# X of steps 2 and 3 from TensorE products, the first six steps in a new order, and the early loads on SyncE's queue

## The chip, the cores and the metric

The kernel runs on one core of one Trainium2 chip. The metric is the time of one execution on the device in microseconds (us). The profile is that of one execution; its engines are named PE (TensorE), PEld (TensorE's weight loads), DVE (VectorE), ACT (ScalarE), POOL (GpSimd) and SP (SyncE, which here only issues transfers).

## What is computed

A delta-rule recurrence over 768 tokens for 4 batches of 8 heads of width 48, and an MLP with a hard-swish over its 3072 x 384 output.

```python
# q, k, v: (4, 8, 768, 48), beta: (4, 8, 768), all of them converted where they come as float64
k_n = k / (norm(k, axis=-1) + 1e-6)
for t in range(768):
    y[:, :, t] = q[:, :, t] @ state                       # (48) x (48 x 48), per batch and head
    state = state + beta_t * outer(k_n_t, v_t - k_n_t @ state)
x = y as (3072, 384)                                      # heads side by side
h = x @ w_in                                              # w_in 384 x 2048
out = (h * clip(h + 3, 0, 6) / 6) @ w_out                 # w_out 2048 x 384
```

q, k, v and beta are float32; the two weights are read as 64-bit numbers, in 16 pieces of 768 KB, and turned into float32 on the chip.

## The kernel before

**The recurrence in blocks.** A step takes 32 tokens of all four batches (128 partitions), so there are 24 steps. Within a step the recurrence is a triangular system. Its inverse, called X, is built from the strictly triangular products of the keys, and overwrites them in the tile LB. With X the step is a few small products, and only the state passes from step to step.

**What a step consists of.**
- `norms` (L337): the norms of the keys of a group of steps (sq, ss, root, some small operations, inv).
- `prep` (L378): GpSimd makes the normed keys kb (L383), the masks mb (L391) and the scaled keys bkb (L438); TensorE transposes keys and queries (pt, L409); ScalarE copies them to KQ (L412); TensorE multiplies them (sc, L425); VectorE masks the result into LB (L434).
- X, in one of two ways. `product` (L457) builds it from products on TensorE (pi, L485) with transposes, copies and sums between them on VectorE and ScalarE; it does one step, and takes TensorE's time. `inverse` (L551) takes a whole group of four steps to DRAM and back in another layout (A), eliminates column by column with 60 operations (pr, L566; A, L571), each needing the one before it, and brings X back through DRAM.
- `chain` (L601): ks (state times keys and queries, L622), R (L635), pz (X times R, L643), Z (L685), then su (the state's change, L710), py (L643), the new state (L726), y (L735), and in `seam` the transpose of y to xT (yt, L699).

**The MLP.** Two steps make a block of 256 tokens. `up` (L750) makes a unit of three products ph (L760) for each 128 columns of w_in, ScalarE's t (L765) and VectorE's g (L772). `down` (L788) makes products po with w_out (L795) for the first two blocks, `down_by_seven` (L836) a form with seven products for four for the others (L856). A piece of weights is converted by `scales` (five passes on ScalarE, L298) and `convert` (three on VectorE, L317, L322, L327) before it can be used. The converted pieces of w_in serve two units each.

**The order.** Everything is issued by hand. The string ORDER lists the first part as words: each word takes the next piece of one of the generators (p5 the next piece of step 5's prep, h2 of step 2's chain, x0 of step 0's product, i1 of group 1's inverse, n norms, k, q, v and w loads, a and c the two halves of a weight's conversion, u the next unit of the MLP, g VectorE's part of a unit that waits for it). All engines run their instructions in the order in which they are issued. From step 6 on a loop lays 15 units beside each step's chain and the preps of steps further on.

**Groups.** Steps 0 and 1 form group 0 and get X from `product`; steps 2 to 5 are group 1, 6 to 9 group 2, and so on up to 22 and 23; all these get X from `inverse` on VectorE. Before ORDER starts, the keys of six steps, queries of four, values of two and all pieces of w_in are issued, on SyncE's queue and partly on ScalarE's.

Of the kernel before, what the change touches and what calls it, by code (L numbers as in the profile page):

```python
# [22 lines left out]
n0*8 n1 p0 n1 p0 n1 p0 q*2 p0 q p1 q p1 n1 p0 p1 a n1 a*2 p0 q*2 a*2 c a q p1 x0 n1*2 a n1*3 a  # L23
p2*2 x0 q c k2 p2 a p1 p3 x1 c p3*2 p2 a x1*2 p2 p4 p1 a*2 x1 k2*2 p3 p2 a*3 p3 k2 p5 x0 c*2
k2*3 p3 x0 c a*4 x0 k2 c*3 p4 p5 k2*2 x1 k2 x0 p4 c*2 p5 p4 p5 p4*2 p5 x1*2 k2 x0 p5 a x1 a i1 c
x0 x1 a x0 c x1 k2 x1 x0*2 k2 c i1 v k2 i1 x1 i1 x0 i1*2 a i1*2 x0 q i1*3 a i1 h0*2 i1*3 q i1*3
h0 i1*3 v i1 x1 i1 q i1 h0 i1*3 a i1*2 a h1 a*2 h1 i1*2 h0 i1 h1 q h1 i1 c i1 v h1*2 v i1 h1 k2
i1*5 v i1 v i1 v c w v i1 a c a*2 i1 a i1 c i1 v q i1 a v*2 i1 v a c i1*4 w i1*2 h1 n2 i1*4 a
i1*3 a i1 h2 i1*2 c a i1 a i1 n2 a c*2 u a g c n2 a c u a n2 g u n2*3 a n2 q c a g n2*2 a c a p6
h2 u h2 c p6 a w p6 u q*2 a v g q*2 a h2 p6 c q*2 v u p7 a q p6 a q p7 p6 v p8 c g q h2 v h2 a c  # L30
w a p7 a k3 h3 u k3 p8 u a h2*2 k3 c g k3 g c h3 c h3 p8 a u k3 a k3 p7 u g q p8 u q w k3 p7 h3
a p9 p8 c a p9 k4 g p9 k4 p7 a*2 g u k3 k4 c k4 h3 a h3 p9 c w k3 k4 k3 a p9 g*2 h3 a c h4 k4 k3
u a h3 c g k4 h4 k3 c w u p8 k3*2 g k3 h4 k3 q a n3 a c n3 c a n3 u q u g u h4 a g p9 a c k4 h4
c a n3 a u a w k4 i2 w*2 a*2 u n3 a h4 v h5 h4 c a u c g n3 c n3*2 g v*2 u h4 n3 u v n3 u c p10
q a*2 q g k4 v q i2 p11 k4 u k4*4 p10 i2*2 q*2 i2*2 k4 u v i2*2 h5 v g h5 i2 a i2 q i2 p10 u h5
u v i2*2 q u i2*2 c i2 p10 g u i2 p10 i2*4 p11 p10 h5*2 q u q h5 p11 g u p11 i2 u i2*2 p12 i2 g
i2*2 p11*2 u i2*2 u i2*3 g i2 u*2 g i2 u*2 g u g u*2 g u i2*6 u*4 h5
# [4 lines left out]
def kernel(  # L42
# [34 lines left out]
    CB = 2  # L77
    TB = CB * P
    assert N % CB == 0 and CB <= GS

# [6 lines left out]
    NPC, NPM = 2, 4  # L87
    psC = ctx.enter_context(tc.tile_pool(name="psC", bufs=NPC, space=PSUM))
    psM = ctx.enter_context(tc.tile_pool(name="psM", bufs=NPM, space=PSUM))
# [43 lines left out]
    def load_k(t, eng=nc.sync):  # L133

        g, i = group(t)
        if i == 0:
            needs(*(("kb", first(g - 2) + j) for j in range(size(g - 2) if g >= 2 else 0)))
            kfs[g] = stage.tile([P, GS, H, D], FP32, name="kf", bufs=2)
        for b in range(B):
            eng.dma_start(out=kfs[g][rows(b), i], in_=tokens(k, b, t))  # L140
            if b == B - 1:
                past.add(("k", t))
            yield

    def load_q(t, eng=nc.sync):
        if t < N:
            if t >= NQB:
                needs(("qT", t - NQB))
            for b in range(B):
                eng.dma_start(out=qbufs[t % NQB][rows(b), :, 0:D], in_=tokens(q, b, t))  # L150
                if b == B - 1:
                    past.add(("q", t))
                yield
# [3 lines left out]
    def load_v(t):  # L157
        if t < N:
            if t >= NVF:
                needs(("R", t - NVF))  # L160
            vfs[t] = stage.tile([P, H, D], FP32, name="vf", bufs=NVF)
            for b in range(B):
                nc.sync.dma_start(out=vfs[t][rows(b)], in_=tokens(v, b, t))
                if b == B - 1:
                    past.add(("v", t))
                yield
# [61 lines left out]
    places = const.tile([128, 6], FP32, name="places")  # L228
    for i, value in enumerate((1152 - 7.5 / 16, -1600.0, -448.0, -704.0, 704.0 * 128, 1e-30)):
        nc.vector.memset(places[:, i : i + 1], value)  # L230
    powers = (
        (ACTF.Relu, 1.0 / 16), (ACTF.Abs, 1.0), (ACTF.Relu, 1.0), (ACTF.Abs, 1.0),
        (ACTF.Relu, -128.0),
    )
# [53 lines left out]
    def scales():  # L288

        for i in range(NW):  # L290
# [5 lines left out]
            d, z = raws[i], like(es[i % 2], i)  # L296
            for n, (func, scale) in enumerate(powers):
                nc.scalar.activation(  # L298
                    out=z, in_=z if n else d.bitcast(I16)[:, :, :, 3], func=func,
                    bias=places[:, n : n + 1], scale=scale,  # L300
                )
                if n == len(powers) - 1:
                    past.add(("scale", i))
                yield
# [32 lines left out]
    def norms(g, i0, n):  # L337
# [17 lines left out]
        nc.scalar.activation(out=root[:], in_=ss[:], func=ACTF.Sqrt, bias=places[:, 5:6])  # L355
# [14 lines left out]
        for i in range(n):  # L370
            invs[first(g) + i0 + i] = inv[:, i, :]
        yield
# [5 lines left out]
    def prep(t, dma):  # L378
# [3 lines left out]
        needs(*([("bkb", t - NKB)] if t >= NKB else []))  # L382
        nc.gpsimd.tensor_tensor(  # L383
# [17 lines left out]
        for j, src in enumerate((kb, qb)):  # L401
# [3 lines left out]
            ring("pm", NPM, ("pt", t, j))  # L405
            read(("pt", t, j))
            pt = psM.tile([128, NP, P], FP32, name="pt", tag="pm")
# [38 lines left out]
        if g > 0:  # L446
# [3 lines left out]
            dma.dma_start(  # L450
# [6 lines left out]
    def product(t, pool):  # L457
# [6 lines left out]
        needs(("bkb", t))  # L464
# [3 lines left out]
        VY = pool.tile([P, 2, H * C], FP32, name="VY", bufs=CB)  # L468
        V, Y = VY[:, 0, :], VY[:, 1, :]
        T = pool.tile([P, H * C], FP32, name="VT", bufs=CB)  # L470
        F = pool.tile([P, H * C], FP32, name="F", bufs=CB)
# [3 lines left out]
        def times(rhs):  # L475
# [3 lines left out]
            ring("pm", NPM, key)  # L479
            keys.append(key)  # L480
            ps = psM.tile([P, 2, H * C], FP32, name="pi", tag="pm")
# [69 lines left out]
    def inverse(g, dma, back):  # L551
# [5 lines left out]
        dma.dma_start(  # L557
# [4 lines left out]
        for j in range(1, C - 1):  # L562
# [3 lines left out]
            nc.vector.tensor_tensor(  # L566
# [4 lines left out]
            nc.vector.tensor_tensor(  # L571
# [3 lines left out]
        nc.vector.memset(A.rearrange("p c i -> p (c i)")[:, 0 : C * C : C + 1], -1.0)  # L575
        back.dma_start(
# [4 lines left out]
        for i in range(size(g)):  # L581
            yield
            LBv = LBs[first(g) + i][:].rearrange("p e a j w -> p (e a) j w")
            back.dma_start(out=LBv[:, :, 0, :], in_=x_dram[g][i].rearrange("h p c -> p h c"))
# [16 lines left out]
    def chain(t):  # L601
# [78 lines left out]
        ring("pm", NPM, ("pz", t))  # L680
        read(("pz", t))
        pz = psM.tile([P, 512], FP32, name="pz", tag="pm")
# [6 lines left out]
        def seam():  # L689

            blk, cc = divmod(t, CB)
# [3 lines left out]
            ring("pm", NPM, ("yt", t))  # L695
            read(("yt", t))
            pt = psM.tile([128, NKT, P], FP32, name="yt", tag="pm")
# [21 lines left out]
        ring("pm", NPM, ("py", t))  # L719
        py = psM.tile([P, 512], FP32, name="py", tag="pm")  # L720
# [29 lines left out]
    def up(blk):  # L750

        needs(*(("seam", blk * CB + i) for i in range(CB)))
        xT = xTs[blk]
        for f in range(NFC):
            needs(("w", f * 128 // WP))
            settle(2)
            ring("pm", NPM, ("ph", blk, f))
            ph = psM.tile([128, TB], FP32, name="ph", tag="pm")
# [23 lines left out]
    def to_dram(t, o):  # L782
        for b in range(B):
            r0 = b * S + t * C
            eng = nc.scalar if t >= N - CB and b % 2 else nc.sync
            eng.dma_start(out=out[r0 : r0 + C, :], in_=o[rows(b ^ 1)])

    def down(blk, c, f0):  # L788

        needs(("w", NWI + f0 // WF))  # L790
        if f0 == 0:
            ring("pm", NPM, ("po", blk, c))
            pos[c] = psM.tile([128, DM], FP32, name="po", tag="pm")
# [5 lines left out]
        if f0 + WF == NFC:  # L799
            if c == 0:  # L800
                pos["o"] = mlp[0].tile([128, CB, DM], FP32, name="o", bufs=1)
# [3 lines left out]
            to_dram(blk * CB + c, o)  # L805
# [14 lines left out]
    assert 2 * WP * NKT == HF * HM and CB == 2 and HF % 2 == 0  # L820
# [15 lines left out]
    def down_by_seven(blk):  # L836
# [8 lines left out]
        o = mlp[0].tile([128, CB, DM], FP32, name="o", bufs=1)  # L845
        u = mlp[0].tile([128, HM], FP32, name="u", bufs=1)[:]
        C11, C12, C21, C22 = (o[:, c, m : m + HM] for c in range(CB) for m in (0, HM))
# [264 lines left out]
```

## Time and profile before

| | |
|---|---|
| time, median of 3 | 724.28 us (723.74 to 726.2) |
| span of the profiled execution | 725.1 us |
| TensorE busy | 656.7 us (91%) |
| VectorE busy | 454.9 us (63%) |
| ScalarE busy | 247.3 us (34%) |
| GpSimd busy | 89.5 us (12%) |
| transfers | 44.72 MB, mean 62 GB/s |

The busy shares are means over a span whose beginning and rest differ much, so the questions are where TensorE is not busy, and what it waits for there. The profile gives for each instruction its start and its duration, and for the idle time before it the event that ended it. The clock that TensorE was granted is given per stretch, 1.00 being full speed.

### The profile page before, as it was taken

Reading aid. Unit: us, or ns where it says so; the run is one execution under the profiler, and the core shown is the slowest. Engines: PE = TensorE matmul, PEld = TensorE weight load, DVE = VectorE, ACT = ScalarE, POOL = GpSimd, SP = SyncE. Lnnn points to the kernel's source line nnn. Section 1 sums busy time; section 2 is a strip of 40 time slices with the busy share of each in tenths; the row PEclk is TensorE's granted clock in tenths of the full one; section 3 lists DMA queues with packets and bytes.
Section 4 is the critical chain, followed back from the end, with each engine's and each line's share of the span. In section 5 each row is a group of like instructions: output and inputs, shape, how many; then the busy total and the mean of one; then the engine's idle time right before and its main releaser. Section 6 shows DMA issues by size and latency. Waiting matters only on the chain.

```text
span 725.1 us, 25019 instructions
## 1 busy us (share of the span) xinstructions
PE 656.7 (91%) x10984; PEld 571.9 (79%) x10984; DVE 454.9 (63%) x1209; ACT 247.3 (34%) x467; POOL 89.5 (12%) x128
## 2 busy tenths in 40 slices
PE   0666839798979999999999999999999999999997
PEld 0455627666756789889889899898898898989997
DVE  6556996488583379665489464598444894533343
ACT  1763688593130331331322322322313213222130
POOL 3640024004031101041110031000000000000000
PEclk9966569899999999999999999999999999999999
DMA  7954437472042312421410411212302001000000
GB/s 135 298 119 89 112 91 176 90 183 37 8 96 48 75 32 42 90 36 26 96 32 15 98 33 31 52 21 60 53 2 50 13 16 39 2 24 1 23 1 22
DMA packets 135853, 44.72 MB, mean 62 GB/s; under 512 B 126112, under 2 KB 129184, under 8 KB 135744
## 3 DMA queue, kind: packets, MB, share of 16 engines
q1 hardware_dynamic: 126832, 40.99, 25.4%
q10 hardware_dynamic: 8912, 2.13, 1.5%
q8 instruction: 86, 1.41, 0.8%
q14 instruction: 23, 0.19, 0.1%
HBM read 32.60 MB, written 10.49 MB: 59 GB/s over the span
## 4 chain that ended last, share of the span: by engine, by line
PE 78%; issue 7%; DVE 5%; DMA 4%; POOL 2%; ACT 2%; SPq 1%; POOLq 0%; DVEq 0%
PE ph L760 31%; PE po L856 26%; PE po L795 3%; PE pz L643 3%; PE ks L622 3%; PE su L710 3%; PE py L643 3%; PE pt L409 3%; PE sc L425 2%; DMA kf<-in_k_dram 2%; DMA spare<-in_moe_w_in_dram 1%; PE pi L485 1%; ACT spare L298 1%; DMA vf<-in_v_dram 1%; PE yt L699 1%
## 5 line engine op out<-in xcount | busy, mean ns | idle before, releaser
L760 PE MATMUL ph<-xT,w_in 128*128 128x256 f32 x1152 | 269.6, 386 | 2.6 <-issue 2.3
L760 PEld LDWEIGHTS ph<-xT,w_in 128*128 128x128 f32 x1152 | 216.4, 193 | 34.7 <-issue 3.0
L765 ACT ACTIVATE t<-ph,halves 128x256 f32<-128x256 f32 x192 | 90.8, 474 | 207.3 <-PE ph L760 204.6
L772 DVE SCALAR_TENSOR_TENSOR g<-t,ph 128x256 f32<-128x256 f32 x192 | 79.8, 418 | 120.5 <-ACT t L765 120.3
L856 PE MATMUL po<-w_out,g 128*128 128x192 f32 x640 | 111.9, 327 | 0.0
L856 PEld LDWEIGHTS po<-w_out,g 128*128 128x128 f32 x640 | 104.2, 190 | 0.5
L856 PE MATMUL po<-spare,g 128*128 128x192 f32 x480 | 87.2, 330 | 0.0
L856 PEld LDWEIGHTS po<-spare,g 128*128 128x128 f32 x480 | 78.0, 190 | 1.2
L298 ACT ACTIVATE spare<-spare,places 128x768 uint16<-128x768 uint16 (+1 forms) x74 | 69.2, 940 | 7.7 <-DVE w_in L327 3.3
L566 DVE TENSOR_TENSOR pr<-A 128x30 f32<-128x30 f32 (+19 forms) x180 | 62.8, 349 | 4.1
L571 DVE TENSOR_TENSOR A<-A,pr 128x30 f32<-128x30 f32 (+19 forms) x180 | 61.9, 344 | 4.1
L842 DVE TENSOR_TENSOR g<-g 128x256 f32<-128x256 f32 x160 | 60.4, 428 | 3.7 <-PE po L856 3.5
L409 PE MATMUL pt<-ident,kb 128*128 128x128 f32 x96 | 18.3, 326 | 32.8 <-POOL kb L383 32.8
L795 PE MATMUL po<-w_out,g 128*128 128x384 f32 x128 | 45.4, 494 | 0.0
L383 POOL TENSOR_TENSOR kb<-kf,inv 128x384 f32<-128x384 f32 x24 | 23.5, 979 | 176.0 <-DVE inv L369 73.0
L412 ACT ACTIVATE KQ<-pt 128x512 f32<-128x512 f32 x48 | 28.2, 594 | 47.4 <-PE pt L409 47.4
L409 PEld LDWEIGHTS pt<-ident,kb 128*128 128x128 f32 x96 | 13.8, 167 | 36.0 <-POOL kb L383 33.8
L863 ACT ACTIVATE o<-po 128x192 f32<-128x192 f32 x40 | 13.2, 331 | 82.8 <-PE po L856 79.7
L391 POOL TENSOR_TENSOR mb<-beta_tok,mask 128x256 f32<-128x256 f32 x48 | 33.8, 724 | 56.2 <-DVE LB L434 56.2
L726 DVE TENSOR_TENSOR state<-state,su 128x384 f32<-128x384 f32 x46 | 23.3, 548 | 22.2 <-PE su L710 22.2
L795 PEld LDWEIGHTS po<-w_out,g 128*128 128x128 f32 x128 | 23.5, 192 | 12.9 <-issue 0.5
L635 DVE SCALAR_TENSOR_TENSOR R<-ks,parity,vf 128x192 f32<-128x192 f32 x46 | 16.9, 410 | 26.3 <-PE ks L622 26.2
(97 smaller groups left out, 581.5 us busy)
## 6 DMA issues: line engine op xcount, KB each, us to landing
spare<-in_moe_w_out_dram SPq DMA_DIRECT2D x8, 768.0 KB, 5.4
vf<-in_v_dram SPq DMA_DIRECT2D x96, 48.0 KB, 2.6
qb<-in_q_dram SPq DMA_DIRECT2D x92, 48.0 KB, 2.4
out_dram<-o SPq DMA_DIRECT2D x92, 48.0 KB, 1.6
kf<-in_k_dram SPq DMA_DIRECT2D x84, 48.0 KB, 2.8
w_out<-in_moe_w_in_dram SPq DMA_DIRECT2D x4, 768.0 KB, 9.6
LB<-x_dram SPq DMA_DIRECT2D x22, 128.0 KB, 3.1
x_dram<-A SPq DMA_DIRECT2D x5, 512.0 KB, 2.8
```

Source lines behind the costliest of these rows:

```text
L298: nc.scalar.activation(out=z, in_=z if n else d.bitcast(I16)[:, :, :, 3], func=func, bias=places[:, n : n + 1], scale=scale,)
L391: nc.gpsimd.tensor_tensor(out=mb[:, e], in0=beta_tok[:, t, e:H:2].unsqueeze(2).unsqueeze(3).to_broadcast([P, NP, 2, C]), in1=mask2[:].unsq ...
L409: nc.tensor.transpose(pt[:, p, :], src[:, 2 * p : 2 * p + 2].rearrange("p e w -> p (e w)"), ident[:])
L566: nc.vector.tensor_tensor(out=pv, in0=A[:, j, j + 1 :].unsqueeze(1).to_broadcast([n, j, w]), in1=A[:, 0:j, j].unsqueeze(2).to_broadcast([n ...
L571: nc.vector.tensor_tensor(out=A[:, 0:j, j + 1 :], in0=A[:, 0:j, j + 1 :], in1=pv, op=ALU.subtract)
L643: nc.tensor.matmul(ps[rows(place(b)), D * h : D * h + D], lhsT=m(h)[rows(b)], rhs=z[rows(b), D * h : D * h + D], start=True, stop=True, sk ...
L760: nc.tensor.matmul(ph[:], lhsT=w_in[:, s, f * 128 : (f + 1) * 128], rhs=xT[:, s, :], start=(s == 0), stop=(s == NKT - 1),)
L765: nc.scalar.activation(out=t1[:], in_=ph[:], func=ACTF.Relu, bias=half, scale=1.0 / 6.0)
L772: nc.vector.scalar_tensor_tensor(out=g, in0=t1[:], scalar=1.0, in1=ph[:], op0=ALU.min, op1=ALU.mult)
L795: nc.tensor.matmul(pos[c][:], lhsT=gs[blk, f // 2][:, f % 2, c * P : (c + 1) * P], rhs=w_out[:, f, :], start=(f == 0), stop=(f == NFC - 1),)
L842: nc.vector.tensor_tensor(out=A(f, *out), in0=A(f, *a), in1=A(f, *b), op=op)
L856: nc.tensor.matmul(ps[n][:], lhsT=A(f - f % 2, *a)[:, f % 2], rhs=b[:, f], start=(f == 0), stop=(f == HF - 1),)
```

## The change

Group 0 grows from two steps to four (CB 4; the MLP's blocks of two steps are now BK): steps 2 and 3 also get X from `product`. Groups are then 0 to 3, 4 to 7, 8 to 11 and so on, one fewer in all. The inverse of group 1 (steps 4 to 7) is done by GpSimd, the others by VectorE as before. ORDER is written anew; the loads that stood before it are words in it (q, k, v, w), in the order in which their data is used, on SyncE's queue, or on ScalarE's for a word in capitals (four of them). Norms of steps 0 and 1 are taken one step at a time (words m0, m1), and step 0's kb is made by VectorE. A weight's scale is made in three passes on ScalarE for five. Tiles of `product` have two buffers each; the first part has three PSUM banks in the place of four, and the fourth is set aside for products without a purpose that would fill TensorE's gaps (word z), of which this ORDER has none.

```diff
-    CB = 2
-    TB = CB * P
+    CB, BK = 4, 2
+    TB = BK * P
...
-    NPC, NPM = 2, 4
+    NPC = 2
...
+    psM, NPM = [None], [3]
...
-            for n, (func, scale) in enumerate(powers):
-                nc.scalar.activation(
-                    out=z, in_=z if n else d.bitcast(I16)[:, :, :, 3], func=func,
-                    bias=places[:, n : n + 1], scale=scale,
-                )
...
+            nc.scalar.activation(
+                out=z, in_=d.bitcast(I16)[:, :, :, 3], func=ACTF.Relu,
+                bias=places[:, 0:1], scale=1.0 / 16,
+            )
+            yield
+            nc.scalar.activation(
+                out=w, in_=z, func=ACTF.Prelu, bias=places[:, 1:2], scale=-1.0, alpha=TINY
+            )
+            yield
+            nc.scalar.activation(
+                out=z, in_=w, func=ACTF.Prelu, bias=places[:, 2:3], scale=-128.0 / TINY, alpha=TINY
+            )
...
-        nc.gpsimd.tensor_tensor(
+        (nc.vector if t == 0 else nc.gpsimd).tensor_tensor(
             out=kb[:, :, 0:D], in0=kfs[g][:, i],
...
-        VY = pool.tile([P, 2, H * C], FP32, name="VY", bufs=CB)
+        VY = pool.tile([P, 2, H * C], FP32, name="VY", bufs=2)
...
-    def inverse(g, dma, back):
+    def inverse(g, eng):
...
-            nc.vector.tensor_tensor(
+            eng.tensor_tensor(
                 out=pv, in0=A[:, j, j + 1 :].unsqueeze(1).to_broadcast([n, j, w]),
...
-            for t in range(LA):
-                drain(load_k(t, nc.scalar if t % 2 else nc.sync))
-                if t == 1:
-                    drain(load_q(0))
-                    drain(load_q(1, nc.scalar))
-            for t in range(CB, NQB):
-                drain(load_q(t))
-            for i in range(3):
-                load_w(i, early if i < 2 else stage)
-            for t in range(CB):
-                drain(load_v(t))
-            for i in range(3, NWI):
-                load_w(i)
...
+        return made(("i", g), lambda: inverse(g, nc.gpsimd if g == 1 else nc.vector), g < NG)
...
+            psM[0] = first_steps.enter_context(
+                tc.tile_pool(name="psM3", bufs=NPM[0], space=PSUM)
+            )
+            psI = first_steps.enter_context(tc.tile_pool(name="psI", bufs=1, space=PSUM))
+            idle.append(psI.tile([128, 128], FP32, name="idle"))
...
+                queue[0] = nc.scalar if word[0].isupper() else nc.sync
+                word = word.lower()
+                if word == "z":
+                    busy()
...
-            needs(("X", 0), ("X", 1), ("w", 0), ("w", 1))
+            needs(*(("X", t) for t in range(CB)), ("w", 0), ("w", 1))
```

The beginning of the new ORDER, up to the first transposes, and its first words around the first unit:

```
q K0 k0 q Q q k0 K0 w Q k0 q k0 m0 k0*2 m0*3 q m0 m1*7 q a m0*2 a p1 p0 c a k1 k0 q*2 c p1 c k1
...
p6 x3 x2 p6 c x3 a p6 x2 x3 a x2 v k3*2 p6 x3 x2 a c a x2 u g k2 q h2 c k2 k3 c u g i1 c h2 a k2
```

Lines of the changed kernel used below: pi is L498, pt L422, ph L773, and the two operations of the inverse are L579 and L584.

## The prediction

> **What bounds the kernel now.** I read the slices of the page first, then the busy times by stage, then TensorE's timeline at the edges of the stages.
>
> ```profile
> PE   0666839798979999999999999999999999999997
> ...
> PEclk9966569899999999999999999999999999999999
> ...
> L298 ACT ACTIVATE spare<-spare,places 128x768 uint16<-128x768 uint16 (+1 forms) x74 | 69.2, 940 | 7.7 <-DVE w_in L327 3.3
> ```
>
> A slice is 18.1 us. TensorE stands at nines from the thirteenth slice (217 us) on; before that it has gaps, and from 36 to 109 us its clock is 0.5 to 0.6. L298, ScalarE's passes over the weights (80 with all their forms, 0.94 us each), lies wholly in that early part. The stages, in the busy times by stretch:
>
> ```profile
> core 0: us, PE busy (x) PEld busy (x) DVE busy (x) ACT busy (x) POOL busy (x), PEclk, DMA share, GB/s
> 16.00:88.00 72.00, 47.95 (x1719) 40.58 (x1720) 50.69 (x112) 42.39 (x59) 20.72 (x24) 0.72 0.61 161
> 88.00:108.00 20.00, 7.44 (x32) 6.32 (x32) 19.05 (x50) 14.92 (x23) 3.08 (x4) 0.67 0.31 68
> 108.00:170.50 62.50, 54.28 (x1187) 42.34 (x1185) 41.89 (x84) 45.44 (x72) 16.42 (x21) 0.93 0.61 141
> 170.50:215.30 44.80, 41.16 (x523) 30.32 (x524) 32.77 (x86) 11.46 (x24) 8.98 (x11) 0.96 0.18 40
> 215.30:725.00 509.70, 505.89 (x7526) 452.34 (x7526) 301.29 (x836) 131.33 (x290) 36.51 (x48) 1.00 0.18 37
> ```
>
> From 215.3 on TensorE is busy 505.9 of 509.7 us at clock 1.00: that stage is its own work, and nothing outside it can shorten it. Before that, there is no product for 16 us, then 48 us of work in 72 at clock 0.72, 7.4 in 20, 54 in 62.5, 41 in 45: some 65 us idle, and part of the busy time is work at a slow clock. Time can be won or lost only here.
>
> ```profile
> 68.27 0.88 PE L643 MATMUL pz<-vf,LB 32*32 32x48 f32 x36 [1.70 <-DVE LB L543]
> ...
> 87.60 6.09 PE L760 MATMUL ph<-xT,w_in 128*128 128x256 f32 x24
> 106.25 1.11 PE L409 MATMUL pt<-ident,kb 128*128 128x128 f32 x4 [12.56 <-POOL kb L383]
> ...
> 113.27 0.60 PE L409 MATMUL pt<-ident,kb 128*128 128x128 f32 x4
> ...
> 215.32 0.94 PE L643 MATMUL pz<-R,LB 32*32 32x48 f32 x36 [3.36 <-DVE g L772]
> ```
>
> Columns: start, us, engine, line, operation, count, and in brackets the idle time before and what ended it. 68.27 is the first use of a finished X (step 0), 87.60 the first product with w_in; after its four units (a unit is three products, six records) TensorE stands 12.56 us for step 6's keys. 113.27 is the same four transposes as 106.25, 0.60 against 1.11 us: the clock. 215.32 is pz of step 6, the first step of the main loop.
>
> **The marker.** I counted TensorE's instructions in the two built orders up to pz of step 6. They are the same (52 + 52 transposes at pt, 384 sc, 96 ph, 36 po, and six steps of pz, su, py, ks, yt), save for pi: 384 before, 768 after. So the remaining 509.8 us hold for both, and the new time is (when pz of step 6 starts) + 509.8.
>
> [...]
>
> ```profile
> 66.32 0.19 DVE L571 TENSOR_TENSOR A<-A,pr 128x30 f32<-128x30 f32 x1
> ...
> 164.87 0.75 DVE L571 TENSOR_TENSOR A<-A,pr 128x30 f32<-128x30 f32 x1
> ```
>
> 0.19 us for the same instruction alone, 0.75 us beside GpSimd's kb and mb. GpSimd's own durations (min/median/max):
>
> ```profile
> L391 POOL TENSOR_TENSOR mb<-beta_tok,mask x48: 609/616/1324, 16.3 to 450.1; 128x256 f32<-128x256 f32 x48
> ```
>
> ```profile
> L383 POOL TENSOR_TENSOR kb<-kf,inv x24: 826/831/1424, 15.3 to 442.8; 128x384 f32<-128x384 f32 x24
> ```
>
> [...] a Prelu pass is taken at L298's 0.94 us. [...]
>
> ```profile
> 8.89 4.76 ACTq L140 DMA_DIRECT2D kf<-in_k_dram  x8
> 13.70 0.31 ACT L355 ACTIVATE root<-ss,places 128x16 f32<-128x16 f32 x1 [11.39 <-DMA kf<-in_k_dram]
> ```
>
> ScalarE issues eight key loads until 13.65 us, and the first root waits 11.39 us behind them.
>
> **The change part by part.**
>
> *Loads.* Twelve key and four query loads leave ScalarE's queue, four stay; loads come in order of use, weights later. ScalarE still issues beta until 3.4 us and then its four, so step 0's keys land near 7.5 us (issue 4.9 + 2.3, the landing of L140). Step 1's come behind one weight piece, near 9.5. Norms (sq 0.56, ss 0.55, root 0.31, five small ops of 0.2) give kb near 13 us, against 15.3. This is worth 2 to 3 us; bandwidth isn't the limit later (v of step 0 ends the first 5.5 MB; the kernel before had moved 5.6 MB by 30 us: 155 GB/s for 20, 336 and 165 for five each).
>
> *Scales.* 3 passes for 5: 48 for 80, so 32 x 0.94 = 30 us of ScalarE, in a stretch where it was busy 42 of 72 and 45 of 62 us. No path of its own; it shortens waits of pt and pi for ScalarE (2.9 + 2.8 + 1.4 us).
>
> *X of steps 0 and 1.* They start at 19 and 22 us (LB): four groups of transposes 4.3 us, KQ copies of 0.6, two sc of 1.2, LB 0.69. One product alone is 1.65 (four set-up ops) + 4 x 0.93 + 2 x 1.93 on TensorE + about 3.8 on VectorE and ScalarE + 11 hand-overs of 0.26 (the idle time of ScalarE between TensorE's pt and KQ) = 16 us. Two interleaved, with norms of steps 4 to 7 (5.8) and a conversion among them on VectorE, take about 22: first pz at 44.5, against 68.3, where other work stood between the parts.
>
> *From there to the first w_in product.* TensorE's new order holds, at the slow durations of this trace: the chains of steps 0 and 1 (pz 1.67, su 1.3, py 1.5, yt 0.9, and a ks of 1.96: 14.7 us), transposes of six steps (12 groups of 1.07: 12.9), six sc (7.2), and X of steps 2 and 3 (2 x 7.6 = 15.2): 50 us. VectorE has 38 us beside it. Following the waits by hand, instruction by instruction with these durations, gives 54 us; the profile shows a further 4.7 us of instruction supply before pi, and GpSimd's contention some 2. First unit at 44.5 + 60.5 = 105 (98 if neither shows, 113 to 119 if TensorE stays at its present share of 48 in 72). That is 17 us later than now, but with X of steps 0 to 3, preps of 0 to 7 and six to eight pieces of w_in done, so no hole of 12.56 us follows.
>
> *Units, step 2 on.* To pz of step 4: 26 units of 1.3 us, two chains of 3.9 at full clock, six groups of transposes of 0.5, two sc of 0.8: 46 us. VectorE has about 41 to 48 in the same stretch (20 g of 0.41, 19 conversion ops, two R/y, norms), so little stands.
>
> *X of steps 4 to 7 on GpSimd.* 60 dependent ops over 9920 columns. From 616 ns for 256 and 831 for 384: 0.19 + 1.68 ns a column, so 28 us; step 8's prep among them 2.9; times 1.18, the mean over the median of mb and kb (724/616, 979/831), 36.5; and hand-overs of 0.05 (0.4 us idle before the eight of L192): 40. Bounds: 31 with no contention, 55 if half of them take twice their time, as mb's maximum of 1324 does. It starts 8 us after step 6's LB (56.8 to 63.7 and the issue before it, in this trace), near 110, ends at 150. Behind it on GpSimd queue kb of steps 9 and 10, and TensorE's pt of step 9 stands before pz of step 4 in its order: due at 146 (105 + 41), released at 150, 4 us of wait. The way back through DRAM is 5.9 us (96.42 to 102.3), so pz of step 4 at 156 instead of 151. What VectorE gains: 21 us that stood at 66 to 97.
>
> *Step 5 and 6.* One unit and two sc cover little of the chain pz, Z, su, state, ks, R: 8 us, pz of step 5 at 164. Then 23 units (29.8) and 4.9 of chain and transposes: 35. VectorE has 36 before R of step 6 (50 ops of the next inverse 16.4, ten g, nine conversions) with GpSimd's preps against it, which stretch small two-input ops as shown: 3 us more. Pz of step 6 at 202; but X of step 6 is there by then, and the 3.36 us wait of now is gone with the group. 202 + 509.8 = 711.8 on the profiled span, about 711 as timed (725.1 against 724.28).
>
> *Small edits* (buffers by two, three PSUM banks, an idle bank with no instruction in it, first kb on VectorE): nothing by themselves: kb 0.56 us on VectorE for 1.03 on GpSimd, once; with three banks for four a product waits for an older reader, and the readers stand before it in the order. One inverse fewer over the whole run (21 us of VectorE) is hidden beside TensorE.
>
> **The rivals.** *GpSimd late.* Contention at the upper bound, inverse 52 instead of 40 us: pz of step 4 moves by 12, of which VectorE's 3 are absorbed: 720. For it: 0.75 for 0.19 us; against: the medians lie at the minimum. *Cold and tangled, slower.* TensorE's gaps stay empty and it keeps its share of the stretch (48 of 72, 0.67): 50/0.67 = 75 us, first unit at 119, and the inverse 9 us late too: 711 + 14 + 9 = 734. For it: the same short products, one after another, now for four steps; against: the waits seen there were for ScalarE passes and loads that the change removes. *Better.* First unit at 98 and an inverse of 31: no wait at step 4, pz of step 5 at 153, of step 6 at 188: 698.
>
> **How the numbers follow.** Main case 0.60 at 711, better 0.10, GpSimd late 0.18, slower 0.12. Faster than 722.1 are the first two and half of the third, 0.79; within 0.3% most of the rest of it, 0.07; slower 0.14. The range goes from the better case to a little beyond GpSimd late, 698 to 728; outside it lies the slower case and little else.
>
> **What would show it.** Right: first pz near 44, first L773 near 105 with no long hole after it, pz of step 4 released by X's way back or by kb of step 9, pz of step 6 near 202, and 510 us from there. Wrong: pi or pt waiting over 10 us between 45 and 105 (the slower rival), GpSimd's L579 and L584 at a mean over 0.8 us (late), VectorE full with conversions where g is waited for, or a main loop that isn't 510 us.

## The result and the profile after

The changed kernel takes 733.4 us (median of 4, 732.2 to 735.3) against 725.0 for the one before: a ratio of 1.012, 95% interval 1.009 to 1.015. It is slower; 711 was predicted. From the page of the kernel after, tenths of busy time and of granted clock in 40 slices of 18.3 us, then the row of the products of X, then the transfers of TensorE's own instructions (packets, MB, share):

```profile
PE   1647788958899999999999999999999999999997
...
PEclk9657779977999999999999999999999999999999
...
q8 instruction: 92, 1.51, 0.9%
...
L498 PE MATMUL pi<-VY,VT 32*32 32x32 f32 (+1 forms) x1280 | 26.5, 247 | 16.1 <-issue 12.4
```

TensorE is at nines from the twelfth slice on (201 us), with a hole at the ninth (146 to 164 us) where the kernel before had one at the sixth. The pi row has 16.1 us of idle time before these products, 12.4 of them "issue", that is with no event that the profile shows as its end. Before pz of step 0 the "issue" waits are 12.6 us, and up to the first unit 20.0; in the kernel before, where X of two steps is made so, they were 4.7 before products of X.

TensorE's timeline of the kernel after, at the milestones that the prediction named (start, us, engine, line, operation, records, and in brackets the idle time before and what ended it):

```profile
54.27 1.50 PE L656 MATMUL pz<-vf,LB 32*32 32x48 f32 x63
...
107.34 1.56 PE L773 MATMUL ph<-xT,w_in 128*128 128x256 f32 x6 [1.12 <-DVE LB L556]
...
160.96 1.11 PE L422 MATMUL pt<-ident,kb 128*128 128x128 f32 x4 [7.35 <-POOL kb L396]
...
169.15 0.88 PE L656 MATMUL pz<-R,LB 32*32 32x48 f32 x64
...
183.52 0.88 PE L656 MATMUL pz<-R,LB 32*32 32x48 f32 x64
...
220.77 0.88 PE L656 MATMUL pz<-R,LB 32*32 32x48 f32 x64
```

| start, us | before | predicted | after | after, kb of steps 8 to 10 on VectorE |
|---|---|---|---|---|
| pz of step 0 | 68.3 | 44.5 | 54.2 | 53.5 |
| first product with w_in | 87.6 | 105 | 107.3 | 106.9 |
| pz of step 4 | 149.5 | 156 | 169.2 | 160.0 |
| pz of step 5 | 170.5 | 164 | 183.5 | 173.2 |
| pz of step 6 | 215.3 | 202 | 220.8 | 210.3 |
| from there to the end | 509.8 | 509.8 | 509.6 | 509.8 |

So nearly the whole difference arises before step 6. From the first unit to pz of step 6 the new order needs 113.4 us where the old one needed 127.7, a gain of 14.3; but the first unit comes 19.7 us later. The last column is the experiment that turned the loss into a gain. What GpSimd did meanwhile, in its timeline of the kernel after:

```profile
111.36 0.23 POOL L579 TENSOR_TENSOR pr<-A 128x30 f32<-128x30 f32 x1 [22.26 <-DMA A<-l_dram]
...
129.40 0.61 POOL L579 TENSOR_TENSOR pr<-A 128x240 f32<-128x240 f32 x1
134.48 0.83 POOL L396 TENSOR_TENSOR kb<-kf,inv 128x384 f32<-128x384 f32 x1 [4.46 <-DVE inv L381]
135.27 2.22 POOL L404 TENSOR_TENSOR mb<-beta_tok,mask 128x256 f32<-128x256 f32 x2
137.45 1.41 POOL L584 TENSOR_TENSOR A<-A,pr 128x240 f32<-128x240 f32 x1
...
160.00 0.16 POOL L588 MEMSET A<- 128x32 f32 x1
160.07 0.83 POOL L396 TENSOR_TENSOR kb<-kf,inv 128x384 f32<-128x384 f32 x1
```

The inverse runs from 111.4 to 160.1, 48.7 us. In the middle of it stands kb of step 8, which waits 4.46 us for VectorE's norms and holds the inverse with it: the inverse's next operation at 137.45 needs only the one that ended at 130.0, and starts behind kb and mb, in the order of issue. Right behind its last operation comes kb of step 9, and that is what TensorE's pt at 160.96 waited for. This wait does not depend on when the units begin: in three runs below whose first unit comes at 98.0, 109.4 and 117.4 us it is 7.35 or 7.36 us too. TensorE's wait passes on: ScalarE has a copy of that pt next in its order, and VectorE's next conversion stands 8.88 us for ScalarE (its timeline, at 163.57).

### The profile page after: what moved, and what is told of

Its sections match the earlier page's. It is cut to its first block, busy times and chain, and to the rows that moved or that the text cites. A ratio compares the mean times of both kernels' runs of the same rounds, so it can differ in the third digit from the quotient of the medians.

```text
span 730.4 us, 26493 instructions
## 1 busy us (share of the span) xinstructions
PE 665.3 (91%) x11752; PEld 580.4 (79%) x11752; DVE 435.7 (60%) x1119; ACT 222.2 (30%) x440; POOL 122.2 (17%) x186
## 3 DMA queue, kind: packets, MB, share of 16 engines
q8 instruction: 92, 1.51, 0.9%
## 4 chain that ended last, share of the span: by engine, by line
PE 84%; issue 5%; POOL 3%; DVE 3%; SPq 2%; DMA 2%; ACT 1%; POOLq 0%; DVEq 0%
PE ph L773 32%; PE po L869 26%; PE po L808 5%; PE pi L498 3%; PE ks L635 3%; PE py L656 3%; PE su L723 3%; PE pz L656 3%; PE pt L422 3%; PE sc L438 2%; POOL A L584 1%; SPq L145 1%; PE yt L712 1%; POOL pr L579 1%; SPq L157 1%
## 5 line engine op out<-in xcount | busy, mean ns | idle before, releaser
L773 PE MATMUL ph<-xT,w_in 128*128 128x256 f32 x1152 | 265.4, 382 | 3.6 <-issue 1.5
L773 PEld LDWEIGHTS ph<-xT,w_in 128*128 128x128 f32 x1152 | 213.6, 190 | 34.9 <-issue 1.9
L404 POOL TENSOR_TENSOR mb<-beta_tok,mask 128x256 f32<-128x256 f32 x48 | 35.9, 767 | 60.1 <-DVE LB L447 51.8
L396 POOL TENSOR_TENSOR kb<-kf,inv 128x384 f32<-128x384 f32 x23 | 20.6, 896 | 150.9 <-PE pt L422 91.8
L579 DVE TENSOR_TENSOR pr<-A 128x30 f32<-128x30 f32 (+14 forms) x120 | 43.0, 358 | 2.5
L584 DVE TENSOR_TENSOR A<-A,pr 128x30 f32<-128x30 f32 (+14 forms) x120 | 41.3, 344 | 2.7
L498 PE MATMUL pi<-VY,VT 32*32 32x32 f32 (+1 forms) x1280 | 26.5, 247 | 16.1 <-issue 12.4
L422 PE MATMUL pt<-ident,kb 128*128 128x128 f32 x96 | 18.5, 329 | 23.5 <-POOL kb L396 23.5
L498 PEld LDWEIGHTS pi<-VY,VT 32*32 32x32 f32 x1280 | 23.3, 141 | 19.3 <-issue 16.8
L808 PEld LDWEIGHTS po<-w_out,g 128*128 128x128 f32 x128 | 24.0, 194 | 14.3 <-DVE w_out L339 0.8
L422 PEld LDWEIGHTS pt<-ident,kb 128*128 128x128 f32 x96 | 14.1, 170 | 25.8 <-POOL kb L396 24.3
```

The costliest lines, as they stand in the source:

```text
L404: nc.gpsimd.tensor_tensor(out=mb[:, e], in0=beta_tok[:, t, e:H:2].unsqueeze(2).unsqueeze(3).to_broadcast([P, NP, 2, C]), in1=mask2[:].unsq ...
L422: nc.tensor.transpose(pt[:, p, :], src[:, 2 * p : 2 * p + 2].rearrange("p e w -> p (e w)"), ident[:])
L498: nc.tensor.matmul(ps[rows(b), 0:n, w], lhsT=T[rows(b), w], rhs=rhs[rows(b), :, w], start=True, stop=True, skip_group_check=True, tile_pos ...
L579: eng.tensor_tensor(out=pv, in0=A[:, j, j + 1 :].unsqueeze(1).to_broadcast([n, j, w]), in1=A[:, 0:j, j].unsqueeze(2).to_broadcast([n, j, w ...
L584: eng.tensor_tensor(out=A[:, 0:j, j + 1 :], in0=A[:, 0:j, j + 1 :], in1=pv, op=ALU.subtract)
L773: nc.tensor.matmul(ph[:], lhsT=w_in[:, s, f * 128 : (f + 1) * 128], rhs=xT[:, s, :], start=(s == 0), stop=(s == NKT - 1),)
```

## The experiments

Four theories. **One:** the inverse on GpSimd, with kb of step 8 inside it and kb of step 9 behind it, is the main loss. **Rival to it:** VectorE and TensorE are as full there, and other waits stand right behind. **Two:** TensorE's cold clock (0.68 in the mean from 15 to 107 us), since its gaps stay empty. **Three:** TensorE's supply of instructions, the idle time called "issue". All edits are to the changed kernel unless another is named. Each ratio is to the kernel before on the same chip, where that took 726.5 to 728.3 us; so ratios compare best from run to run.

**The inverse on VectorE.**

```diff
-lambda: inverse(g, nc.gpsimd if g == 1 else nc.vector)
+lambda: inverse(g, nc.vector)
```

> Group 1's inverse runs on VectorE instead of GpSimd, at the same places of the order; all else is the changed kernel (733.4 us; pz of step 4 at 169.2, pt of step 9 waits 7.35 us for GpSimd's kb). Theory 1 (the late inverse on GpSimd, with kb of step 9 behind it, is the main loss): the wait at pt of step 9 goes, pz of step 4 comes at 158 to 162, total 722 to 726. Rival (VectorE is as full as GpSimd there: 23.6 of 29 us busy from 125 to 154, and 60 operations of 0.36 us = 21 us come on top): pz of step 4 at 167 or later, total 731 to 738.

734.4 us, ratio 1.011 (1.006 to 1.015): as slow as the change. Its timeline of TensorE has no wait of 7 us for GpSimd, but others, and pz of step 4 is no earlier:

```profile
157.65 4.26 PE L808 MATMUL po<-w_out,g 128*128 128x384 f32 x8 [3.90 <-DVE w_out L339]
...
170.76 0.88 PE L656 MATMUL pz<-R,LB 32*32 32x48 f32 x64
```

The busy times by stretch show why. First the kernel after, then this one (stretch, its length, then for PE, PEld, DVE, ACT and POOL the busy us and instructions, clock, DMA share, GB/s):

```profile
125.00:154.00 29.00, 27.64 (x241) 21.58 (x239) 23.55 (x48) 19.94 (x37) 22.66 (x31) 1.00 0.56 133
```

```profile
125.00:154.00 29.00, 25.06 (x224) 19.60 (x222) 27.91 (x70) 12.98 (x27) 8.90 (x10) 0.94 0.31 68
```

VectorE goes from 23.6 to 27.9 of 29 us, and the conversions of w_out come late. The rival held for this edit: at these places of the order VectorE was no better a place for the inverse. An order laid out for it was not tried.

**Keys of steps 8, 9 and 10 on VectorE.** The inverse stays; only what shares its queue is moved.

```diff
-(nc.vector if t == 0 else nc.gpsimd).tensor_tensor(   # kb
+(nc.vector if t in (0, 8, 9, 10) else nc.gpsimd).tensor_tensor(
```

> kb of steps 8, 9 and 10 is made on VectorE, so that the inverse on GpSimd no longer holds 4.5 us for step 8's norms and TensorE's pt of step 9 no longer stands behind the inverse's end; the inverse stays on GpSimd. Theory 1: the inverse ends near 155 instead of 160, pt of step 9 starts near 154, pz of step 4 waits for X of step 4 to come back and starts near 164, total 728. Rival (other waits stand right behind, nothing is won): pz of step 4 at 168 to 170, total 732 to 734.

723.1 us, ratio 0.996 (0.994 to 0.998): faster than both kernels, by three operations of VectorE. TensorE's timeline:

```profile
153.37 0.66 PE L422 MATMUL pt<-ident,kb 128*128 128x128 f32 x4 [0.19 <-DVE kb L396]
...
159.95 0.88 PE L656 MATMUL pz<-R,LB 32*32 32x48 f32 x64 [0.77 <-DMA LB<-x_dram]
```

pt of step 9 waits 0.19 us and takes 0.66 us in the place of 1.11, the inverse ends at 154.4, and X of step 4 comes back just as TensorE has got to it. pz of step 4 is 9.2 us earlier, 4 more than theory one said: TensorE no longer slows down behind the wait (from pt of step 9 to pz of step 4 its clock was 0.63 in the kernel after; here the four groups of transposes there take 0.60 to 0.66 us each, and the clock from 154 to 172 us is 0.91).

**Each half of it.** Only kb of step 8 moved, `t in (0, 8)`:

> Only kb of step 8 is made on VectorE; kb of steps 9 and 10 stay on GpSimd behind the inverse. Making all three on VectorE brought pz of step 4 from 169.2 to 160.0 us and the profiled span from 730.4 to 720.1. If the hold inside the inverse (4.46 us until step 8's norms are done) is what counts, pt of step 9 waits some 3 us instead of 7.35, pz of step 4 comes at 164 to 165 and the span is near 726. If only the place of kb of step 9 behind the inverse counts, pt of step 9 still waits 7 us and the span is 729 to 731.

Only kb of steps 9 and 10 moved, `t in (0, 9, 10)`:

> Only kb of steps 9 and 10 are made on VectorE; kb of step 8 stays on GpSimd, among the operations of the inverse, with its hold of 4.46 us. pt of step 9 is free at 154, and TensorE does the 5 us of transposes, sc and products that stand before pz of step 4 while the inverse ends (160) and X comes back (5.4 us): pz of step 4 at 165 to 166, waiting for X, span near 726. If the place behind the inverse is all that counts, it comes at 160 to 161 and the span is 720 to 722.

727.2 us, ratio 1.002 (1.000 to 1.003), and 731.1 us, 1.006 (1.004 to 1.008). TensorE's timelines, of the first and of the second:

```profile
159.33 0.66 PE L422 MATMUL pt<-ident,kb 128*128 128x128 f32 x4 [1.89 <-POOL kb L396]
165.07 0.88 PE L656 MATMUL pz<-R,LB 32*32 32x48 f32 x64
```

```profile
153.96 0.66 PE L422 MATMUL pt<-ident,kb 128*128 128x128 f32 x4 [0.39 <-DVE kb L396]
167.17 1.50 PE L656 MATMUL pz<-R,LB 32*32 32x48 f32 x64 [7.41 <-DMA LB<-x_dram]
```

The first unit starts at different times (110.85 and 107.85 here; the profiled execution of the first kernel took 731.3 us, near the upper end of its 724.9 to 731.6), so the stretch from it to pz of step 4 is the fair measure: 61.8 us in the changed kernel, 54.2 with the hold gone, 59.3 with the release, 53.1 with both. The hold inside the inverse is the larger part. With the release alone TensorE runs ahead and waits 7.41 us for X itself. Of the two expectations, that for the hold was near (pt waits 1.89 us where 3 were expected, pz of step 4 at 165.07). That for the release was right in its mechanism, but pz of step 4 came 1 to 2 us later, and the span was 728.3 where 726 was expected.

**Pieces of the weights later.** The five loads of 768 KB that are issued between 34 and 41 us now stand behind the keys of group 2.

```diff
-k1 w n1*2 q n1 v x0 n1 v*2 w a n1*2 v n1 v w n1*3 v w*2 a
+k1 n1*2 q n1 v x0 n1 v*2 a n1*2 v n1 v n1*3 v a
...
-p2 k2 h1
+p2 k2 w*5 h1
```

> Five pieces of w_in (768 KB each) are issued after the keys of group 2 (56 us) instead of at 34 to 41 us; no engine's instructions change but SyncE's. Theory 3 (TensorE's instruction supply is held up by the loads: 12.6 us of idle time with no releaser before pz of step 0, while the DMA engines are 0.73 to 0.89 busy): two thirds of these waits go, pz of step 0 comes at 45 to 48 instead of 54.2, and the total falls by 2 to 8 us unless the same waits come back between 56 and 70 us. Rival (these waits have to do with the many short products themselves, 64 of them per group, not with the loads): pz of step 0 stays at 53 to 55, total 732 to 735.

734.7 us, ratio 1.011 (1.005 to 1.016): nothing won. But the waits lie elsewhere, as TensorE's timeline of this kernel shows:

```profile
50.09 1.32 PE L656 MATMUL pz<-vf,LB 32*32 32x48 f32 x64
...
63.18 0.36 PE L656 MATMUL pz<-R,LB 32*32 32x48 f32 x12 [3.16 <-issue]
69.48 0.48 PE L723 MATMUL su<-Z,bkb 32*64 32x48 f32 x13 [3.30 <-issue]
...
109.39 2.93 PE L773 MATMUL ph<-xT,w_in 128*128 128x256 f32 x6 [1.12 <-DVE LB L556]
```

Before pz of step 0 the "issue" waits fall from 12.6 to 7.2 us and it comes 4.1 us earlier; from there to the first unit they rise from 7.4 to 16.9. The busy times by stretch, kernel after:

```profile
22.00:50.00 28.00, 14.19 (x640) 12.74 (x640) 16.21 (x40) 7.29 (x12) 0.00 (x0) 0.59 0.93 245
55.00:75.00 20.00, 14.90 (x610) 12.80 (x605) 12.16 (x24) 7.90 (x14) 7.58 (x11) 0.76 0.51 125
```

and with the pieces later:

```profile
22.00:50.00 28.00, 15.68 (x771) 14.26 (x765) 18.16 (x48) 7.47 (x12) 0.00 (x0) 0.53 0.53 113
55.00:75.00 20.00, 9.77 (x402) 8.21 (x401) 9.72 (x19) 6.25 (x10) 5.11 (x6) 0.74 0.93 266
```

In this pair, whichever stretch has the DMA engines at 0.93 gets fewer records through TensorE: 640 for 771 in the first, 402 for 610 in the second. That the loads are the cause isn't shown by it. The kernel with kb of step 8 alone on VectorE has the same loads and the same order of TensorE as the change, and its profile splits the waits in the same way: 6.4 us before pz of step 0, which comes at 50.2, and 14.6 from there to the first unit at 110.85. Its busy times by stretch:

```profile
22.00:50.00 28.00, 15.53 (x752) 14.04 (x756) 19.28 (x49) 7.53 (x12) 0.52 (x2) 0.57 0.87 223
55.00:75.00 20.00, 13.70 (x509) 11.79 (x509) 10.89 (x22) 6.74 (x11) 4.28 (x5) 0.67 0.57 130
```

752 records at a DMA share of 0.87: early waits and late ones trade places from one profile to another without a load being moved. What loads cost the supply stays open. That the waits could come back later was in the expectation; pz of step 0 at 50.1 lies between its two cases.

**Why "issue" waits: the blocks.** TensorE's timeline of the kernel after, around 45 us:

```profile
36.81 0.39 PE L498 MATMUL pi<-F,VT 32*32 32x32 f32 x11 [0.24 <-DVE VT L539]
40.69 0.91 PE L498 MATMUL pi<-F,VT 32*32 32x32 f32 x51 [3.49 <-issue]
41.37 0.32 PE L498 MATMUL pi<-VY,VT 32*32 32x64 f32 x2
41.41 0.24 PE L498 MATMUL pi<-F,VT 32*32 32x32 f32 x2
41.46 2.23 PE L498 MATMUL pi<-VY,VT 32*32 32x64 f32 x73
48.26 1.71 PE L498 MATMUL pi<-VY,VT 32*32 32x64 f32 x53 [4.57 <-issue]
50.91 1.25 PE L498 MATMUL pi<-VY,VT 32*32 32x32 f32 x74 [0.95 <-DVE VY L551]
53.52 0.91 PE L498 MATMUL pi<-VY,VT 32*32 32x32 f32 x51 [1.36 <-issue]
```

From one such wait to the next are 51 + 2 + 2 + 73 = 128 and 53 + 74 = 127 records. The page counts 92 packets and 1.51 MB on the queue of TensorE's instructions, 16.4 KB each, for 11752 products and as many weight loads: 23504/92 = 255 to a packet. In the kernel before there are 86 packets for 10984 products and as many weight loads, again 255. All five "issue" waits before pz of step 0 end behind such a packet: in the trace of after, packets land at 29.4, 33.3, 39.2, 46.7 and 52.3 us, and TensorE goes on at 31.1, 34.8, 40.7, 48.3 and 53.5, 1.2 to 1.7 us after each. So these are waits for instructions. The times at which it goes on are 5.6 us apart in the mean; with the pieces later (25.6 to 44.1 us) 4.6, with kb of step 8 moved (31.4 to 49.5 us) 4.5. What sets this distance no run shows.

**Filling the gaps.** 48 products of the identity ahead of the first transposes, and three each after 24 groups of pi, 72 more.

```diff
-a m0*2 a p1 p0 c a
+a m0*2 a z*48 p1 p0 c a
...
-q p0 x1 k1 k0
+q p0 x1 z*3 k1 k0
```

> TensorE gets products of the identity with itself into the idle bank (the word z): 48 before the first transposes of step 0, and three after each of six groups of products of X of steps 0 to 3 (72). Theory 2 (the cold clock is the loss): the first transposes take 0.60 instead of 1.11 us, granted clock from 15 to 107 us rises from about 0.7 to 0.9, pz of step 0 near 49, first product with w_in near 100, total 726 to 728. Rival (instruction supply, which more instructions make worse, or waits for VectorE): pz of step 0 at 53 or later, first product with w_in at 106 to 110, total 732 to 737.

And the 48 alone, together with the keys on VectorE:

> kb of steps 8, 9 and 10 on VectorE, and 48 products of the identity into the idle bank ahead of the first transposes only, where TensorE stands for the first keys anyway (in the run with 120 of them these took 13.8 us, from 2 to 15.7). Theory 2 in its narrow form (warm clock where it costs nothing): the first transposes take 0.6 instead of 1.11 us and sc 0.86 instead of 1.19, the chain of X starts 2 us earlier, pz of step 0 at 50 to 52 and the total 720 to 722, 1 to 3 us less than with the keys alone (723.1). Rival (TensorE's instructions come in blocks at their own pace, so what starts earlier waits longer): total 722 to 726.

738.0 us, ratio 1.015 (1.011 to 1.020), and 729.4 us, 1.002 (1.000 to 1.004), where the keys alone gave 0.996. Both came out slower than either of their expectations. In the first, TensorE's clock did rise; its busy times from 15 to 107 us, in the kernel after and in this one:

```profile
15.00:107.00 92.00, 62.64 (x2630) 54.31 (x2630) 58.24 (x120) 33.65 (x54) 25.47 (x31) 0.68 0.54 125
```

```profile
15.00:107.00 92.00, 69.65 (x2461) 60.51 (x2464) 55.05 (x112) 29.72 (x49) 25.38 (x31) 0.85 0.51 121
```

But the filling products stand in TensorE's own order: from 15 us to the first unit they keep it busy for 27.6 us, more than the warmer clock gives back. The first unit comes at 117.4, 10.1 us later, although the "issue" waits fall from 20.0 to 17.5 us. The second kernel's timeline of TensorE:

```profile
15.81 0.66 PE L422 MATMUL pt<-ident,kb 128*128 128x128 f32 x4 [0.25 <-POOL kb L396]
...
54.20 0.49 PE L498 MATMUL pi<-VY,VT 32*32 32x32 f32 x19 [4.85 <-issue]
...
110.57 2.93 PE L773 MATMUL ph<-xT,w_in 128*128 128x256 f32 x6 [1.16 <-DVE LB L556]
```

Behind the 48 products the first transposes take 0.66 in place of 1.11 us. In the kernel before, four such transposes take 1.11 us at a granted clock of 0.50 (106.25 us) and 0.60 at 1.00 (113.27 us); at the first transposes of the kernel after the profile gives 1.00 (15 to 17 us), so that these were slow by the clock is read from their duration alone. It didn't help. 48 products that ran while TensorE stood idle anyway made the kernel slower by 0.6% (some 4 us by the ratios, 6 by the medians), and in the profile the first unit came at 110.6. The clock beyond the first transposes was no warmer: from 15 to 107 us it was 0.67, with the keys alone 0.70. "Issue" waits from 15 us to the first unit are 26.2 us against 19.1 with the keys alone. The products are 96 records, three quarters of a block, and shift all later borders; that this is the cause is a guess, since with kb of step 8 moved a profile without them has 21.0 us of such waits and its first unit at 110.85. So filling the gaps won nothing in either form. What a warm clock alone would be worth in these stages was not measured; in that sense theory two stays open.

**Fewer instructions.** Both edits leave out the separate products for each batch, so what they build is no longer X; only their times are of use, one execution each. First 8 products over all partitions for 32:

```diff
-for b in range(B): matmul(ps[rows(b), 0:n, w], lhsT=T[rows(b), w], rhs=rhs[rows(b), :, w])
+matmul(ps[:, 0:n, w], lhsT=T[:, j : j + P], rhs=rhs[:, :, w])
```

> Each group of products of X of steps 0 to 3 is 8 products over all 128 partitions (128x128 by 128x32) in place of 32 of 32x32; X of these steps is then not the inverse, so the outputs are other numbers. The chain of waits between the groups is the same. Theory 3 (TensorE is supplied with instructions in blocks of 128 records with their weight loads, one per 3.3 to 4 us at best, later ones under load): 288 fewer products for steps 0 and 1 are 4.5 blocks, pz of step 0 at 38 to 44 instead of 54.2, with at most two idle times without a releaser before it, and the first product with w_in at 85 to 95 instead of 107. Rival (the hand-overs between TensorE, VectorE and ScalarE are the length of this stage): pz of step 0 at 50 or later.

then 16 of 64x64 for 32:

```diff
-for b in range(B): matmul(ps[rows(b), 0:n, w], lhsT=T[rows(b), w], rhs=rhs[rows(b), :, w])
+for b in (0, 2): matmul(ps[r, 0:n, w], lhsT=T[r, j : j + 2 * C], rhs=rhs[r, :, w])   # r: 64 rows
```

> Each group of products of X of steps 0 to 3 is 16 products of 64x64 by 64x32 in place of 32 of 32x32, in the changed kernel; X of these steps is then not the inverse, so the outputs are other numbers. By the trace a record of 64x64 by 64x48 (ks, 64 in 1.96 us at the slow clock) takes no longer than one of 32x32 by 32x64 (64 in 1.9), so TensorE's work of the 12 groups before pz of step 0 falls by about half, 7 us, and its instructions by 384 records, three blocks of 128. Theory 3 (supply of instructions): idle time without a releaser before pz of step 0 falls from 12.6 us to 4 or less, pz of step 0 at 38 to 43, and the first product with w_in at 90 to 97 instead of 107. Rival (hand-overs between the engines): the saved work is filled by waits for VectorE, pz of step 0 at 47 or later, the first product with w_in at 100 or later.

TensorE's timelines, of the first:

```profile
24.60 17.25 PE L498 MATMUL pi<-VY,VT 128*128 128x32 f32 x80 [0.84 <-DVE VT L513]
...
63.43 1.50 PE L655 MATMUL pz<-vf,LB 32*32 32x48 f32 x64
```

and of the second:

```profile
42.24 3.63 PE L500 MATMUL pi<-VY,VT 64*64 64x32 f32 x64 [5.50 <-DVE VY L553]
45.80 1.50 PE L658 MATMUL pz<-vf,LB 32*32 32x48 f32 x64
...
98.00 1.56 PE L775 MATMUL ph<-xT,w_in 128*128 128x256 f32 x6 [0.56 <-DVE LB L558]
```

In both no "issue" wait is left before pz of step 0. In the first that gained nothing, since a record with a weight load of 128x128 took 17.25/80 = 0.22 us: pz of step 0 at 63.4, the time 752.4 us, and the expectation was wrong. In the second pz of step 0 came at 45.8, 8.4 us earlier (50.1 to 56.2 in the profiles with all 32 products), the first unit 9.3 us earlier, and the execution took 721.6 us. That lies between the theories: the 12.6 us of supply waits went, but a wait of 5.50 us for VectorE, which had the norms of four steps ahead of that operation, took part of their place. TensorE's time in products of X up to pz of step 0, in the kernel after and in this one, shows what the gain is made of:

```profile
15.00:54.20 39.20, 16.18 (x765) 14.64 (x768) 5.98 (x15) 1.53 (x4) 0.65 0.82 198
```

```profile
15.00:45.80 30.80, 15.90 (x384) 15.11 (x384) 5.91 (x15) 1.54 (x4) 0.85 0.84 199
```

Half as many products took as long, 15.90 us for 16.18; the 7 us of work that were expected to be saved were not. All of TensorE's work in the stretch is 21.9 us in the one and 21.3 in the other, so nearly all of the 8.4 us is waits that went. Theory three holds for the number of instructions; for the loads it is open.

**Pieces one at a time, with the keys.** From the fifth piece on, each behind another key or unit word.

```diff
-n1*2 v n1 v w n1*3 v w*2 a
+n1*2 v n1 v n1*3 v a
...
-k2 p2 k2
+k2 w p2 k2
```

> kb of steps 8, 9 and 10 on VectorE, and the pieces of the weights from the fifth on issued one at a time between the keys of group 2 and the first units, instead of four of them in one go at 36 to 41 us. Theory (loads in a burst hold up the blocks of TensorE's instructions, loads one at a time less): idle time without a releaser from 15 to 107 us falls from some 19 to 12 us, the first product with w_in comes at 100 to 103 and the total is 716 to 720. Rival (the blocks come no faster in the mean, as when five pieces were moved together, or conversions now wait for their pieces): first product with w_in at 106 or later, total 722 to 728.

722.4 us, ratio 0.994 (0.992 to 0.996): with the keys alone it was 0.996 (0.994 to 0.998), which can't be told apart. "Issue" waits from 15 to 107 us are 17.5 us against 19.1. The rival held.

**Three passes alone, in the kernel before.**

```diff
-for n, (func, scale) in enumerate(powers): ...   # five passes
+Relu, Prelu, Prelu as in the change; two of each five words a left out
```

> The kernel before with the three passes of the weights' scales in place of five (two of each five places left out of its order), and nothing else of the change. The prediction gave this part no path of its own: it shortens waits of pt and pi for ScalarE, together 7 us at most. Theory: total 721 to 725, that is 0 to 3 us less than before. Rival (ScalarE's 69 us of passes are on the path of the early part): 716 or less.

722.7 us, ratio 0.994 (0.991 to 0.997). The first unit comes at 87.0 against 87.6 and pz of step 6 at 211.5 against 215.3: 3.8 us, a little over the 0 to 3 us of the expectation.

## Why the prediction was wrong

**The step that failed** is the walk from the first unit to pz of step 5, with X on GpSimd in it. The prediction had 41 us to pt of step 9, a wait of 4, 6 to pz of step 4 and 8 to pz of step 5: 59 us. It took 76.2, and these 17.2 us are nearly all of the 18.6 by which the span is longer. The order of events was right; the terms were too small, and each is given below with what it measured.

**The marker held.** From pz of step 6 to the end it is 509.6 us, and 509.5 to 510.3 in the other runs of the changed order.

**Loads and scales.** GpSimd's first kb starts at 14.65 us, 0.7 earlier than before, for the 2 to 3 predicted: the keys that should be there at 7.5 us were first used at 9.8. The scales had "no path of their own", and alone gave 3.8 us in the kernel before; which waits they shortened was not traced. That a Prelu pass takes L298's 0.94 us was an estimate; the passes of the kernel after took 0.93 to 0.99 us in the mean of each line and form.

**X of steps 0 and 1: 54.2 for 44.5.** The step's sum had TensorE's work, VectorE's and 11 hand-overs, and no term for instruction supply; the walk added 4.7 us for it, after this stage. It was 12.6 us before pz of step 0 alone, 20.0 up to the first unit. The 4.7 us of the old profile were carried over as they stood, although the change doubles the products of X and sets them closer together.

**From there to the first unit: 53.1 for 60.5.** This term was too large, by about what the one before lacked: TensorE's busy time in it is some 40 us, not 50, as the clock was not slow throughout (0.71 in the mean). The 2 us in the term for GpSimd's contention were an estimate that no run shows by itself. The first unit at 107.3 for 105 is thus luck, a hit of two errors of 9.7 and 7.4 us.

**Units: 46.3 us to pt of step 9 for 41.** Units are 1.37 and not 1.3 us, two chains 9.6 and not 7.8, and 2.9 us are waits that were counted at nothing.

**X on GpSimd: a wait of 7.35 for 4, and 8.2 us behind it for 6.** The prediction named the chain of causes, kb of steps 9 and 10 behind the inverse and TensorE's pt of step 9 before pz of step 4. Its 40 us for the inverse were mis-sized: 43.5 where nothing holds it (110.9 to 154.4 in the run with the keys on VectorE), and 48.7 with the hold on step 8's norms. Step 8's prep was priced at 2.9 us of work and not as a wait, although it stood in GpSimd's order between two operations of the inverse. The 6 us behind the wait were X's way back; X was there by then, but TensorE's own work up to pz of step 4 ran at a clock of 0.63 after the pause and took 8.2. Removing the shared queue made the span 10.3 us shorter and turned the sign; all but 0.4 of that lies between the first unit and pz of step 5. This part is shown by experiment. The other 7 us of this stretch are read from the traces alone.

A kb took 0.83 us on GpSimd in the kernel after (the median of 23). The one that VectorE made there, of step 0, took 1.07 us beside GpSimd's of step 1, where the prediction had 0.56; an operation of 128x384 with no GpSimd work beside it, the sq at 9.81 us, took 0.56.

**Steps 5 and 6.** pz of step 5 came 14.4 us after that of step 4 for 8, the largest single error: the working took the chain's length, but TensorE has 11.0 us of its own work in that stretch (transposes, sc, py, ks, a unit, at a clock of 0.76 in the mean) beside 3.3 us of waits, 2.7 of them "issue". Still 13.3 us with the keys moved. Step 6 took 37.2 for 38.

Together: 2.3 us at the first unit, 5.3 in the units, 3.4 for the wait, 2.2 after it, 6.4 at step 5, less 0.8 at step 6 and 0.2 in the rest, 18.6 us.

**The rivals and the signs.** "Slower" had 734 us, and 733.4 was measured, but by luck: it put the first unit at 119 and most of the loss before it, and the first unit came at 107.3. "GpSimd late" had the place and a lateness near the measured one, but not the cause: the operations of the inverse take 0.59 us in the mean, not over 0.8, and it was the hold that made the difference. (Its 52 us don't follow from the working either, which gives 55 for its upper bound.) So none of the signs that the prediction gave for being wrong came: no pi or pt waited over 10 us between 45 and 105, TensorE waited for no g before pz of step 6, and the main loop is 510 us. None of them asked what holds GpSimd inside the inverse, or how much of its own work TensorE has at step 5. Whether a new order could win back the 19.7 us by which the first unit is later was not tried, nor a form of X with fewer products that still gives X.

## What to carry to other kernels

When a long chain of dependent operations moves to another engine, list all that stands in that engine's order within it and behind it: what waits there holds the chain (4.46 us here), and what stands behind it holds whoever is next (7.35 us). Three short operations put elsewhere were worth more here than the place of the chain. And count TensorE's instructions per time, not only its work: hundreds of tiny products outran the supply of instructions here (765 records of pi before the first pz, and 12.6 us of waits). Filled gaps and moved loads did not help; half as many products, with the same busy time, made that stage 8.4 us shorter. Before a difference in a single profile is put down to an edit, look for it in a run that lacks the edit.

## What the runs showed of the hardware

TensorE's instructions came in packets of 16.4 KB, 255 instructions in the mean (92 packets in the kernel after), and 127 or 128 product records lie from one of its waits for them to the next (two cases in the kernel after). Before pz of step 0 it went on from such waits 4.5 to 5.6 us apart in the mean (three runs), 1.2 to 1.7 us after a packet had landed (kernel after). One such wait took 4.85 us (keys on VectorE and 48 products); the profile calls it "issue". A pi record with weights of 128x128 took 0.14 to 0.22 us (16 in 2.25, 80 in 17.25), one with 64x64 0.04 to 0.06 us (64 in 2.27 and in 3.63). GpSimd's 60 dependent operations over 9920 columns took 43.5 us with nothing that held them, and 48.7 with the hold (kernel after, 0.59 us each in the mean).
